# Attention, a two-dimensional Fourier transform and a feed-forward layer on one core: tie weights in PSUM, a norm by columns, ungated value loads and a written plan of finer calls

## The chip, the cores and the metric

The program runs on one core of a Trainium2 chip. The metric is the device time of one execution in microseconds (us). Within the core, TensorE (PE in the profile; PEld is its weight load), VectorE (DVE), ScalarE (ACT) and GpSimd (POOL) compute, and SyncE (SP) issues the transfers.

## What is computed

```python
q_assign = argmax(einsum('bhsd,hcd->bhsc', q_n, c_n), -1)     # likewise k_assign; rows normalised
mask = q_assign[:, :, :, None] == k_assign[:, :, None, :]
scores = where(mask, scale * q @ k.T, -1e9)
attn = softmax(scores) @ v                                    # 4 batches, 8 heads, 768 x 64
x = attn, heads side by side                                  # 4 x 768 x 512
u = x + real(fft(fft(x, axis=1), axis=2))
un = (u - mean(u)) / sqrt(var(u) + 1e-6)
out = u + maximum(un @ w_ch1, 0) @ w_ch2                      # 512 -> 2048 -> 512
```

The two weight matrices arrive as 8-byte floats.

## The kernel before

**Work.** There are 16 pairs of heads (four of each batch), and each has six tiles of scores for either head, 192 of 128x768 in all. A pair goes through four streams. `prep` loads q and k, finds their largest values, sets the scales, splits each into two 16-bit halves, and assigns every row to a cluster. `scores` multiplies (L596, L601), takes the row's extreme on DVE (L615), the exponential on ACT (L618), splits the result into halves (L626 on ACT, L627 on POOL) and transposes it by DMA (L629). `attend` multiplies by the values (L647 to L649), and `load_v` and `split_v` bring the values in and split them (L466, L475 to L477). When the four pairs of a batch are done, its tile X of 768x512 goes through `fold` and `transform` (L908 and L999, matmuls L977) and then through the layer in three blocks of 256 rows: `norm` (L1069), `inverse` (L1101), `up` (L1127, 192 matmuls to a block) and `down` (L1157, 96). A batch's transform and layer fill PE between the scores of the next batches. Behind batch 3 nothing is left to fill with.

**Weights.** In the first 190 us the 32 pieces of the weights (512 KB each) are loaded, their sign and exponent are put together on PE (L767, L791), the rest of the bits is joined on DVE (L795), and the result is halved on ACT, DVE and POOL (L804, L807, L805). The raw pieces lie in `arena`, a stretch of SBUF that the transform and the layer use later.

**Ties.** In `prep`, L547 turns the cluster products into one PSUM bank; L553 takes the largest of each row and L555 compares, after which the bank is free. POOL multiplies by tie weights (L557), L561 takes the largest again into a small SBUF tile `mx2`, and one L565 and two L569 compare with it, 16 and 32 times over the run. Both inputs of these, `a` (tile ac) and `mx2`, lie in SBUF.

**PSUM.** Scores have two buffers of two banks (ps_big), the products with the values one bank (ps_o), and all else shares three banks (ps_f): the turned cluster products, the weights' block and join, the transform, up and down.

**Order.** `Overlap` (L1170) calls the streams by a timetable: every step of a pair has a time, and the transform and the layer are let in by a budget of costs. Each call is marked, and after tracing, `Order` (L77) goes through all instructions with a cost of its own for each and hands every engine, whenever it is free, the instruction of the earliest call whose inputs its costs hold to be ready. So the order on an engine follows from the calls and from `Order`'s costs. `Order` is not changed.

**Values.** From the second or third pair on, `load_v` first copies one number from the newest row extreme (`self.late`) into the value tile on POOL (L465, 14 times). The transfer of the values (L466) waits for that copy, and stands in SP's queue in its place.

**Norm.** For a block's two tiles of 128 rows, `norm` takes the statistics (L1083, L1084) and then does five operations of 128x2 on DVE: the variance plus 1e-6 (L1085), a shift and a mask of its bits (L1086), a subtraction that gives a power of two near its inverse root (L1088), the product with the mean (L1090), and a copy of the variance for `inverse` (L1091). ACT normalises (L1094, L1096), DVE or POOL takes the low half (L1097), and a DMA transposes it for `up`.

Of the kernel before, what the change touches and what calls it, by code (L numbers as in the profile page):

```python
# [56 lines left out]
def top_power(nc, tops, t, s, inv):  # L57

    t = t.bitcast(I32)
    nc.vector.tensor_scalar(out=t, in0=tops.bitcast(I32), scalar1=23, scalar2=None, op0=ALU.logical_shift_right)  # L60
    nc.vector.tensor_scalar(out=t, in0=t, scalar1=-13.0, scalar2=1.0, op0=ALU.add, op1=ALU.max)
    nc.vector.tensor_scalar(out=inv.bitcast(I32), in0=t, scalar1=240.0, scalar2=float(1 << 23), op0=ALU.min, op1=ALU.mult)
    nc.vector.reciprocal(out=s, in_=inv)
# [276 lines left out]
class Arena:  # L340
# [5 lines left out]
    def at(self, off, shape, dt):  # L346
        n = int(np.prod(shape[1:]))
        size = 2 if dt in (F16, BF16, U16) else 4
        assert off % 32 == 0 and off + n * size <= self.t.shape[1] * 4
# [8 lines left out]
class Attention:  # L358
# [9 lines left out]
    def __init__(self, ctx, tc, q, k, v, cent, X, ident, sc, psf, kept):  # L368
# [9 lines left out]
        self.late, self.centered, self.ready, self.mark = None, False, -1, None  # L378
# [103 lines left out]
    def load(self, pr):  # L482
        b, hp = divmod(pr, H // 2)
        t = self.sb.tile([P, 2, S], F32, name="scr", tag="scr")
        for side in range(2):
            self.nc.sync.dma_start(out=t[:, side], in_=(self.q, self.k)[side][b, hp])
        self.nat[pr] = t

    def largest_qk(self, pr):
        m = self.sb.tile([P, 3], F32, name="amx", tag="amx", bufs=2)  # L490
        for i in range(2):
            self.nc.vector.tensor_reduce(out=m[:, i:i + 1], in_=self.nat[pr][:, i], op=ALU.max, axis=AX.X,
                                         apply_absolute_value=True)
        return m
# [11 lines left out]
    def split_qk(self, pr, side):  # L506
# [5 lines left out]
        i = nc.vector.scalar_tensor_tensor(out=hl[:, 1], in0=src, scalar=s, in1=hl[:, 0], op0=ALU.mult, op1=ALU.subtract)  # L512
        if pr == 0:
            self.mark = i
        return hl

    def prep(self, pr):
        nc, sb = self.nc, self.sb
        hp = pr % (H // 2)
        self.load(pr)  # L520
        yield
        m = self.largest_qk(pr)
        yield
        nc.vector.tensor_reduce(out=m[:, 2:3], in_=self.vst[pr].rearrange("p a x -> p (a x)"), op=ALU.max, axis=AX.X,
                                apply_absolute_value=True)
        yield
# [4 lines left out]
        yield  # L531
# [28 lines left out]
        mx2 = sb.tile([P, G], F32, name="mx", tag="mx")  # L560
# [7 lines left out]
        for h in range(2):  # L568
            i = nc.vector.tensor_tensor(out=k[:, :, :, h, 0:NC_], in0=av[:, :, h, 1],  # L569
                                        in1=mv[:, :, h, 1].broadcast_to([P, 3, 2, NC_]), op=ALU.is_equal)  # L570
        if pr == 0:
            self.mark = i
# [8 lines left out]
        self.ready = pr  # L581
# [3 lines left out]
    def scores(self, pr, st):  # L585
        nc, sb = self.nc, self.sb
        assert self.ready >= pr
# [15 lines left out]
        for j in range(2):  # L603
# [11 lines left out]
            self.mark = nc.vector.tensor_scalar(out=ju, in0=ps[j][:, :, 0:SH], scalar1=ne, scalar2=None, op0=ALU.mult, op1=ALU.min,  # L615
                                    accum_out=m)
            self.late = m
# [13 lines left out]
        if st == ST - 1:  # L631
            self.hl.pop(pr)
            self.oht.pop(pr)


    def attend(self, pr, st):
        nc, sb = self.nc, self.sb
        W = D + 2
        if st % 3 == 0:
            self.otile[pr] = self.po.tile([P, 512], F32, name="ps_o")  # L640
        o = self.otile[pr]
        for j in range(2):
            v16, pt = self.v16[2 * pr + j], self.pt.pop((pr, st, j))
            at = (st % 3 * 2 + j) * W
            for kt in range(ST):
                hi, lo = pt[:, kt], pt[:, ST + kt]
                nc.tensor.matmul(out=o[:, at:at + W], lhsT=hi, rhs=v16[:, kt, 0:W], start=(kt == 0), stop=False)  # L647
                nc.tensor.matmul(out=o[:, at:at + D], lhsT=hi, rhs=v16[:, kt, 66:130], start=False, stop=False)  # L648
                nc.tensor.matmul(out=o[:, at:at + W], lhsT=lo, rhs=v16[:, kt, 0:W], start=False, stop=(kt == ST - 1))  # L649
        if st % 3 == 2:  # L650
            self.finish(pr, st // 3)
# [55 lines left out]
class Weights:  # L707
# [7 lines left out]
    RAW, PN = tuple(4128 * i for i in range(6)) + (29696, 33824), (24768, 40000, 44096)  # L715
    ID, TOP, MX, ONE = 28864, 29376, 29472, 29568
    X32 = 37952
    EXTRA, A2, AHEAD = 0, 9, 7

    def __init__(self, tc, pool, arena, psf, w1, w2, ident):  # L720
# [5 lines left out]

        self.inv = [pool.tile([P, 4], F32, name=f"winv{n}") for n in range(2)]
        self.rel = pool.tile([P, 16], F32, name="wrel")
        self.scale, self.bits, self.sum = {}, {}, {}

    def raw(self, k):

        n, e = len(self.RAW), self.EXTRA
        if n <= k < n + e:
            o = 16 * DM - 2064 * ((k - n) // 2 + 1)
            return self.w2[k % 2].rearrange("p a x -> p (a x)")[:, o:o + 4 * DM + 8].bitcast(U16)
        return self.arena.at(self.RAW[(k if k < n else k - e) % n], [P, 4 * DM + 8], U16)

    def loads(self, k):

        n = len(self.RAW) + self.EXTRA
        if k < 0:
            k += self.AHEAD
            return range(n * k // self.AHEAD, n * (k + 1) // self.AHEAD)
        a = min(self.A2, n - 1)
        return [p for p in range(n, 32) if k == p - (a if p < n + len(self.RAW) else len(self.RAW) - 1)]

    def top(self, k):
        raw = self.raw(k)
        return raw[:, 4:4 + 4 * DM].rearrange("p (n f) -> p n f", f=4)[:, :, 0]  # L750

    def load(self, k):
        m, i = divmod(k, 16)
        raw = self.raw(k)
        src = self.src[m][i % 4 * P:(i % 4 + 1) * P, i // 4 * DM:(i // 4 + 1) * DM] if m == 0 else \
            self.src[m][i * P:(i + 1) * P]
        self.nc.sync.dma_start(out=raw[:, 1:1 + 4 * DM], in_=src.bitcast(U16))

    def block(self, g):
# [4 lines left out]
        i = 0  # L764
        for k in range(4 * g, 4 * g + 4):
            for j in range(2):
                nc.tensor.matmul(out=ps, lhsT=self.ones[:, 0:1].broadcast_to([P, P]), rhs=self.bits[k][:, j], start=(i == 0), stop=(i == 7))  # L767
                i += 1
        mx = at(self.MX + 32 * (g % 2), [P, 1], F32)
        nc.vector.tensor_reduce(out=mx, in_=ps, op=ALU.max, axis=AX.X)  # L770
        s = self.sb.tile([P, 1], F32, name="wsc", tag="wsc", bufs=2)
        top_power(nc, mx, ps[:, 0:1], s, self.inv[g // 4][:, g % 4:g % 4 + 1])
        for i in range(4):
            self.scale[4 * g + i] = s[:, 0:1]

    def signs(self, k):

        nc, at = self.nc, self.arena.at
        pn = at(self.PN[k // 2 % 3], [P, 2, 2, DM], BF16)
        raw = at(self.RAW[k % len(self.RAW)], [P, 2, 4 * DM + 16], U16)  # L780
        top = raw[:, :, 4:4 + 4 * DM].rearrange("p a (n f) -> p a n f", f=4)[:, :, :, 0]
        nc.scalar.activation(pn[:, 0].bitcast(I16), top.bitcast(I16), AF.Relu, bias=self.off[:, 0:1], scale=8.0)
        nc.scalar.activation(pn[:, 1].bitcast(I16), top, AF.Relu, bias=self.off[:, 1:2], scale=8.0)
# [600 lines left out]
```

## Time and profile before

| | us |
|---|---|
| three runs | 998.67, 1002.95, 1002.15 |
| median | 1002.15 |
| the profiled execution | 1003.47 |
| its span | 1001.40 |
| outside the span | 2.07 |
| PE busy | 896.3 |
| POOL, ACT, DVE busy | 601.6, 604.3, 599.3 |
| PE idle ahead of 250 us, 250 to 860 us, behind 860 us | 81.6, 15.0, 8.6 |

The profile is one execution. Its span runs from the first to the last recorded instruction, and each engine's busy time is counted on its own. An idle time of PE is put down to what released PE last. Where another engine is on the chain that ended last, its busy time counts as PE's does.

### The profile page before, as it was taken

To read this page: it belongs to the slowest core of one execution; us is meant where nothing else is said; L and a number is where in the kernel's file an instruction comes from. 1 tells how busy PE (TensorE), PEld (TensorE's weight loads), DVE (VectorE), ACT (ScalarE), POOL (GpSimd) and SP (SyncE) were. 2 spreads that over 40 slices of the span, in tenths; PEclk is the share of its full clock that TensorE was granted. 3 is DMA by queue.
4 is the path that set the end of the run, shared out by engine and by line. 5 is a ranking of instruction groups with operands and counts; after the bars stand their busy time and mean duration, and the time that the engine had idled before them with its cause. 6 is when DMAs were issued, how large, how long until landed. Compare 5 with 4: busy or idle time off the path is not lost.

```text
span 1001.4 us, 23416 instructions
## 1 busy us (share of the span) xinstructions
PE 896.3 (90%) x9349; PEld 586.1 (59%) x9368; DVE 599.3 (60%) x1276; ACT 604.3 (60%) x948; POOL 601.6 (60%) x702
## 2 busy tenths in 40 slices
PE   3775768578899999999999999889999999899998
PEld 1243444356666757666757667556658585576683
DVE  7788979789555655879555646767554335611110
ACT  6899989656756756557656656557656352342130
POOL 2467667667866756759857567559757462552230
PEclk9799877778899999999999999999999999999999
DMA  7799999979768666699676666689765552311000
GB/s 263 196 225 256 267 226 238 198 157 179 143 118 175 108 154 134 123 181 212 116 167 118 154 118 143 122 151 180 118 125 109 107 106 59 71 26 33 11 11 22
DMA packets 397374, 140.65 MB, mean 140 GB/s; under 512 B 381904, under 2 KB 382928, under 8 KB 397264
## 3 DMA queue, kind: packets, MB, share of 16 engines
q1 hardware_dynamic: 397264, 139.16, 67.4%
q8 instruction: 73, 1.20, 0.5%
q14 instruction: 37, 0.30, 0.1%
HBM read 43.17 MB, written 6.29 MB: 49 GB/s over the span
## 4 chain that ended last, share of the span: by engine, by line
PE 62%; DVE 14%; ACT 8%; DMA 6%; issue 5%; POOL 4%; SPq 1%; DVEq 0%; ACTq 0%; POOLq 0%
PE ps_f L1157 21%; PE ps_f L1127 20%; PE ps_big L596 7%; PE ps_f L977 3%; PE ps_o L647 2%; PE ps_o L648 2%; PE ps_o L649 2%; DVE ps_big L615 2%; PE ps_big L601 2%; DMA scr<-in_q_dram 2%; DMA pt<-p 1%; ACT p L618 1%; POOL ph L627 1%; DVE X L615 1%; DMA arena<-in_moe_w_ch_dram 1%
## 5 line engine op out<-in xcount | busy, mean ns | idle before, releaser
L627 POOL TENSOR_TENSOR ph<-p,ph 128x768 f16<-128x768 f32 x144 | 241.3, 1678 | 137.0 <-ACT ph L626 101.0
L1127 PE MATMUL ps_f<-arena,w1h 128*128 128x256 f16 x1536 | 267.1, 274 | 11.3 <-ACT arena L1135 11.2
L1157 PE MATMUL ps_f<-w2h,arena 128*128 128x512 f16 x768 | 239.3, 379 | 0.2 <-ACT arena L1135 0.2
L1127 PE MATMUL ps_f<-arena,w1l 128*128 128x256 f16 x768 | 210.7, 274 | 0.0
L618 ACT ACTIVATE p<-ps_big,rmx 128x768 f32<-128x768 f32 x144 | 128.9, 898 | 129.5 <-DVE ps_big L615 82.2
L615 DVE TENSOR_SCALAR_CACHE_REDUCE ps_big<-ps_big,sce 128x768 f32<-128x768 f32 x144 | 142.0, 1020 | 68.8 <-PE ps_big L601 67.5
L1157 PEld LDWEIGHTS <-arena 128*128 128x128 f16 x1152 | 109.0, 98 | 125.9 <-issue 5.0
L1136 POOL TENSOR_TENSOR arena<-arena 128x256 f16<-128x256 f32 x192 | 130.9, 691 | 79.8 <-ACT arena L1135 75.7
L1127 PEld LDWEIGHTS <-w1h 128*128 128x128 f16 x1536 | 151.0, 98 | 23.2 <-issue 4.8
L596 PE MATMUL ps_big<-hlk,hlq 64*128 64x384 f16 x1152 | 127.2, 345 | 22.6 <-ACT p L618 11.8
L1157 PE MATMUL ps_f<-w2l,arena 128*128 128x512 f16 x384 | 145.5, 379 | 0.0
L626 ACT CAST ph<-p 128x768 f16<-128x768 f32 x144 | 118.9, 828 | 27.2 <-DMA pt<-ph 26.9
L647 PE MATMUL ps_o<-v,pt 128*128 128x66 f16 x1152 | 123.7, 198 | 11.5 <-DMA pt<-p 7.5
L648 PE MATMUL ps_o<-v,pt 128*128 128x64 f16 x1152 | 123.6, 199 | 0.0
L649 PE MATMUL ps_o<-v,pt 128*128 128x66 f16 x1152 | 123.2, 197 | 0.0
L647 PEld LDWEIGHTS <-pt 128*128 128x128 f16 x1152 | 109.7, 100 | 22.2 <-DMA pt<-p 8.3
L1132 DVE TENSOR_SCALAR arena<-ps_f,wrel 128x256 f32<-128x256 f32 x96 | 46.3, 482 | 121.4 <-PE ps_f L1127 83.7
L1135 ACT ACTIVATE arena<-ps_f,wrel 128x256 f16<-128x256 f32 x192 | 89.6, 474 | 42.4 <-DVE arena L1132 41.9
L648 PEld LDWEIGHTS <-pt 128*128 128x128 f16 x1152 | 110.1, 100 | 4.6 <-issue 0.8
L649 PEld LDWEIGHTS <-pt 128*128 128x128 f16 x1152 | 110.4, 102 | 0.0
L596 PEld LDWEIGHTS <-hlq 64*128 64x128 f16 x1152 | 54.8, 98 | 81.9 <-issue 55.6
L1127 PEld LDWEIGHTS <-w1l 128*128 128x128 f16 x768 | 75.5, 98 | 21.2 <-issue 12.3
(178 smaller groups left out, 1311.9 us busy)
## 6 DMA issues: line engine op xcount, KB each, us to landing
arena<-in_moe_w_ch_dram SPq DMA_DIRECT2D x32, 512.0 KB, 5.2
scr<-in_q_dram SPq DMA_DIRECT2D x16, 384.0 KB, 3.5
scr<-in_k_dram SPq DMA_DIRECT2D x16, 384.0 KB, 4.3
vst<-in_v_dram SPq DMA_DIRECT2D x16, 384.0 KB, 4.0
out_dram<-arena SPq DMA_DIRECT2D x24, 256.0 KB, 2.2
pt<-ph SPq DMA_TRANSPOSE x168, 3.8
arena<-in_cs_dram SPq DMA_DIRECT2D x12, 192.0 KB, 3.9
arena<-in_ss_dram SPq DMA_DIRECT2D x12, 192.0 KB, 3.9
```

The lines of the kernel that those rows point to most:

```text
L596: nc.tensor.matmul(out=ps[j][:, hf, 0:SH], lhsT=hq[rows[j], a, sl], rhs=hk[rows[j], c, hs], start=(i == 0), stop=False)
L615: self.mark = nc.vector.tensor_scalar(out=ju, in0=ps[j][:, :, 0:SH], scalar1=ne, scalar2=None, op0=ALU.mult, op1=ALU.min, accum_out=m)
L618: nc.scalar.activation(x, ju, AF.Exp, bias=m, scale=-1.0)
L626: nc.scalar.copy(out=ph[:, 0], in_=p32)
L627: nc.gpsimd.tensor_tensor(out=ph[:, 1], in0=p32, in1=ph[:, 0], op=ALU.subtract)
L647: nc.tensor.matmul(out=o[:, at:at + W], lhsT=hi, rhs=v16[:, kt, 0:W], start=(kt == 0), stop=False)
L648: nc.tensor.matmul(out=o[:, at:at + D], lhsT=hi, rhs=v16[:, kt, 66:130], start=False, stop=False)
L649: nc.tensor.matmul(out=o[:, at:at + W], lhsT=lo, rhs=v16[:, kt, 0:W], start=False, stop=(kt == ST - 1))
L1127: nc.tensor.matmul(out=ps.rearrange("p (t x) -> p t x", x=P), lhsT=a[:, dc, fs], rhs=c[:, :, dc], start=(i == 0), stop=(i == 11))
L1135: nc.scalar.activation(hh[:, f], ps, AF.Relu, scale=rel[:, f:f + 1])
L1136: nc.gpsimd.tensor_tensor(out=hl[:, f], in0=r, in1=hh[:, f], op=ALU.subtract)
L1157: nc.tensor.matmul(out=ps, lhsT=a[:, f, ts], rhs=c[:, f], start=(i == 0), stop=(i == 47))
```

## The change

**Tie weights.** `mx2` has no SBUF tile any more; it is written to the 24 columns behind the cluster products in the PSUM bank of L547. The bank stays taken until the last of the three comparisons.

**Norm.** Each of the two columns has its own four operations of 128x1, the copy is gone (`inverse` reads the variance where it lies), and `mv` is three wide. A norm has eight small operations where it had five.

**Values.** The copy of L465 is gone; the transfer waits for its tile alone.

**Calls.** In place of the timetable stands `PLAN`, a text of words: p is prep, s scores, a attend, v values, t transform, n norms, f layer, l weight loads, w conversion, c centroids; the digits name the pair or batch and *n says how many steps. The streams give way more often: q and k load apart, each largest value and each split is a step, scores and attend step by head, the conversion after signs, block, join and halve, and the transform after each of its parts. The pieces of the weights and the transform's tables lie at other places of `arena` (the latter 96 bytes on), and the scales of the second matrix are kept in 16 columns.

```diff
...
-        if self.late is not None:
-
-            nc.gpsimd.tensor_copy(out=t[:, 0, 0:1], in_=self.late)
         nc.sync.dma_start(out=t, in_=self.v[b, :, 2 * hp:2 * hp + 2])
...
     def prep(self, pr):
...
-        self.load(pr)
-        yield
-        m = self.largest_qk(pr)
-        yield
...
+        for i in range(2):
+            self.load(pr, i)
+            yield
+        m = self.sb.tile([P, 3], F32, name="amx", tag="amx", bufs=2)
+        for i in range(3):
+            self.largest(pr, m, i)
+            yield
         self.scales(pr, m)
         yield
-        hl = self.hl[pr] = [self.split_qk(pr, side) for side in range(2)]
+        hl = self.hl[pr] = []
+        for i in range(2):
+            hl.append(self.split_qk(pr, i))
+            yield
...
-        mx2 = sb.tile([P, G], F32, name="mx", tag="mx")
+        mx2 = ps[:, G * NC_:G * NC_ + G]
         nc.vector.tensor_reduce(out=mx2, in_=a, op=ALU.max, axis=AX.X)
...
-        va = sb.tile([P, 2], F32, name="mv", tag="mv", bufs=2)
         s = sb.tile([P, 2, 2], F32, name="rpow", tag="rpow", bufs=2)
+        mv = sb.tile([P, 2, 3], F32, name="mv", tag="mv", bufs=2)
...
-        nc.vector.tensor_scalar(out=mv[:, :, 1], in0=mv[:, :, 1], scalar1=1e-6, scalar2=None, op0=ALU.add)
-        nc.vector.tensor_scalar(out=e.bitcast(I32), in0=mv[:, :, 1].bitcast(I32), scalar1=1, scalar2=0x7F800000,
-                                op0=ALU.logical_shift_right, op1=ALU.bitwise_and)
-        nc.vector.tensor_scalar(out=s[:, 0].bitcast(I32), in0=e.bitcast(I32), scalar1=-1.0, scalar2=float(USC << 23),
-                                op0=ALU.mult, op1=ALU.add)
-        nc.vector.scalar_tensor_tensor(out=s[:, 1], in0=mv[:, :, 0], scalar=-1.0, in1=s[:, 0], op0=ALU.mult, op1=ALU.mult)
-        nc.vector.tensor_copy(out=va, in_=mv[:, :, 1])
-        for j in range(2):
+            nc.vector.bn_aggr(out=mv[:, j, 0:2], in_=st)
+            mean, var, e = (mv[:, j, i:i + 1] for i in range(3))
+            nc.vector.tensor_scalar(out=var, in0=var, scalar1=1e-6, scalar2=None, op0=ALU.add)
+            nc.vector.tensor_scalar(out=e.bitcast(I32), in0=var.bitcast(I32), scalar1=1, scalar2=0x7F800000,
+                                    op0=ALU.logical_shift_right, op1=ALU.bitwise_and)
+            nc.vector.tensor_scalar(out=s[:, 0, j:j + 1].bitcast(I32), in0=e.bitcast(I32), scalar1=-1.0, scalar2=float(USC << 23),
+                                    op0=ALU.mult, op1=ALU.add)
+            nc.vector.tensor_scalar(out=s[:, 1, j:j + 1], in0=mean, scalar1=s[:, 0, j:j + 1], scalar2=-1.0, op0=ALU.mult, op1=ALU.mult)
...
-        return va, s[:, 0], self.rest[:, blk]
+        return mv[:, :, 1], s[:, 0], self.rest[b][:, blk]
...
+    PLAN = """
+p0*2 c v0 p0*4 c l w l v1 p0*3 p1*2 l p0 l p0 p1*3 l*2 p0 v0*2 l*2 p1 s0*2 w*5 p1*2 s0*2 l w*2 v2 s0*2 p1 v1 p2*2 l w*2 l w*2
...
+a15*3 f2*2 s15*2 f2*2 a15*2 f2*4 a15*2 f2*4 a15*3 f2*7 t3*4 f2*2 t3*2 f2 t3*12 f2*2 t3 n3*2 t3*2 f2 t3*3 f3 n3*2 f3*21 n3*2
+f3*50
+"""
...
+        for word in self.PLAN.split():
+            name, _, n = word.partition("*")
+            if name not in streams:
+                streams[name] = self.make[name[0]](int(name[1:] or 0))
+            for _ in range(int(n or 1)):
                 self.order.cut("rest")
-                f(*a)
...
+                next(streams[name])
```

The order on PE is much the same before and after: the same matmuls, in large stretches in the same row, and from the last product of pair 14 to the end without a difference. DVE has 36 instructions more, POOL 14 fewer. Three places show what moves.

DVE at the comparisons with the tie weights of the first pair of batch 1. The operands are written as output, arrow, inputs; X_64 is a stretch of SBUF that holds a score tile here, v the split values, vst the raw values, arena the weights' pieces. Before:

```order
L795 SCALAR_TENSOR_TENSOR ps_f<-arena,ps_f 128x512
L565 TENSOR_TENSOR oh<-ac,mx 128x12x16
L615 TENSOR_SCALAR X_64,rmx<-ps_big,sce 128x768
L807 SCALAR_TENSOR_TENSOR w2l<-ps_f,wsc,w2h 128x512
L569 TENSOR_TENSOR oh<-ac,mx 128x6x16
L615 TENSOR_SCALAR X_64,rmx<-ps_big,sce 128x768
L569 TENSOR_TENSOR oh<-ac,mx 128x6x16
L492 TENSOR_REDUCE amx<-scr 128x1 x2
L524 TENSOR_REDUCE amx<-vst 128x1
```

The same place after:

```order
L563 TENSOR_REDUCE ps_f<-ac 128x24
L496 TENSOR_REDUCE amx<-scr 128x1
L567 TENSOR_TENSOR oh<-ac,ps_f 128x12x16
L496 TENSOR_REDUCE amx<-scr 128x1
L571 TENSOR_TENSOR oh<-ac,ps_f 128x6x16
L620 TENSOR_SCALAR X_64,rmx<-ps_big,sce 128x768
L571 TENSOR_TENSOR oh<-ac,ps_f 128x6x16
L620 TENSOR_SCALAR X_64,rmx<-ps_big,sce 128x768
```

The three comparisons read the bank in place of `mx`, and the largest values of the next pair's q and k, which came behind them together, now stand among them.

POOL at the load of the values for the second pair of batch 1, where batch 0 is folded (L919, L929). Before:

```order
L476 MEMSET v_2993 128x6x2
L929 TENSOR_TENSOR arena<-arena,X_63 1x255
L465 COPY vst<-rmx 128x1
L627 TENSOR_TENSOR ph<-p_2644,ph 128x768
L919 TENSOR_TENSOR arena<-arena 128x3x255
L627 TENSOR_TENSOR ph<-p_2653,ph 128x768
```

After:

```order
L930 TENSOR_TENSOR arena<-arena,X_63 1x255
L919 TENSOR_TENSOR arena<-arena 128x3x255
L475 MEMSET v_2978 128x6x2
L631 TENSOR_TENSOR ph<-p_2637,ph 128x768
L631 TENSOR_TENSOR ph<-p_2646,ph 128x768
```

The copy is gone, and the fold's operation of POOL stands ahead of the subtractions of the two score tiles where it stood between them.

DVE at the second norm of batch 3, behind the last scores. Before:

```order
L1084 BN_AGGR mve<-bst 128x2
L1041 SCALAR_TENSOR_TENSOR arena<-ps_f,vseq,arena 128x257
L1085 TENSOR_SCALAR mve<-mve 128x2
L1086 TENSOR_SCALAR mve<-mve 128x2
L1091 COPY mv<-mve 128x2
L1088 TENSOR_SCALAR rpow<-mve 128x2
L1090 SCALAR_TENSOR_TENSOR rpow<-mve,rpow 128x2
```

After:

```order
L1046 SCALAR_TENSOR_TENSOR arena<-ps_f,vseq,arena 128x257
L1091 TENSOR_SCALAR mv<-mv 128x1
L1089 BN_AGGR mv<-bst 128x2
L1047 SCALAR_TENSOR_TENSOR arena<-ps_f,vseq,arena 128x257
L1092 TENSOR_SCALAR mv<-mv 128x1
L1091 TENSOR_SCALAR mv<-mv 128x1
L1094 TENSOR_SCALAR rpow<-mv 128x1
L1092 TENSOR_SCALAR mv<-mv 128x1
L1096 TENSOR_SCALAR rpow<-mv,rpow 128x1
L1094 TENSOR_SCALAR rpow<-mv 128x1
L1096 TENSOR_SCALAR rpow<-mv,rpow 128x1
```

The first column begins while the second still waits for its statistics, and from there the two take turns.

## Rows read from the trace of the kernel before

**Rows 1.** The page: each engine's busy time, share and instructions.

```profile
PE 896.3 (90%) x9349; PEld 586.1 (59%) x9368; DVE 599.3 (60%) x1276; ACT 604.3 (60%) x948; POOL 601.6 (60%) x702
```

**Rows 2.** Windows: length; busy PE, PEld, DVE, ACT, POOL; clock share; DMA share; GB/s.

```profile
0.00:250.00 250.00, 168.39 (x1967) 100.13 (x1987) 206.71 (x454) 200.56 (x266) 154.25 (x170) 0.85 1.00 220
50.00:125.00 75.00, 50.49 (x686) 30.11 (x694) 63.99 (x143) 72.66 (x94) 50.25 (x45) 0.93 1.16 249
...
300.00:860.00 560.00, 549.60 (x5980) 365.47 (x5977) 336.00 (x701) 332.23 (x544) 361.40 (x403) 0.99 0.69 135
860.00:1001.40 141.40, 132.83 (x918) 89.52 (x916) 27.59 (x57) 38.66 (x85) 48.53 (x80) 1.00 0.10 25
```

**Rows 3.** Timeline of DVE near 170 us: start, duration, instruction, [idle before, releaser].

```profile
168.00 1.20 DVE L565 TENSOR_TENSOR oh<-ac,mx 128x192 bf16<-128x192 f32 x1
...
172.81 1.07 DVE L569 TENSOR_TENSOR oh<-ac,mx 128x96 bf16<-128x96 f32 x1
```

**Rows 4.** Timeline of POOL over the same stretch.

```profile
166.91 2.08 POOL L627 TENSOR_TENSOR ph<-X,ph 128x768 f16<-128x768 f32 x1 [0.96 <-POOL arena L928]
```

**Rows 5.** Single lines over the whole run: shortest, median, longest in ns; first, last start.

```profile
L565 DVE TENSOR_TENSOR oh<-ac,mx x16: 316/368/1611, 22.3 to 749.7; 128x192 bf16<-128x192 f32 x16
L569 DVE TENSOR_TENSOR oh<-ac,mx x32: 243/346/1702, 22.6 to 753.0; 128x96 bf16<-128x96 f32 x32
L555 DVE TENSOR_TENSOR ac<-ps_f,mx x16: 547/558/558, 18.8 to 746.1; 128x384 f32<-128x384 f32 x16
L553 DVE TENSOR_REDUCE mx<-ps_f x16: 548/554/558, 18.2 to 745.5; 128x24 f32<-128x384 f32 x16
L561 DVE TENSOR_REDUCE mx<-ac x16: 530/552/554, 21.0 to 749.1; 128x24 f32<-128x384 f32 x16
```

**Rows 6.** The chain that ended last, in order of time: start, duration, what.

```profile
168.10 0.97 DVE oh L565
...
199.84 0.71 POOL vst L465
200.56 3.12 DMA vst<-in_v_dram
...
673.27 1.59 DVE rpow L1088
```

**Rows 7.** Timeline of all engines around the value load at 200 us.

```profile
191.21 6.45 SPq L629 DMA_TRANSPOSE pt<-ph  x2
...
198.94 1.59 POOL L465 COPY vst<-rmx 128x1 f32<-128x1 f32 x1 [1.20 <-ACT p L618]
...
203.78 0.95 DVE L524 TENSOR_REDUCE amx<-vst 128x1 f32<-128x768 f32 x1 [0.85 <-DMA vst<-in_v_dram]
```

**Rows 8.** Timeline of DVE in norms of batches 0 and 3.

```profile
234.08 1.58 DVE L1085 TENSOR_SCALAR mve<-mve 128x2 f32<-128x2 f32 x1
...
244.13 1.50 DVE L1090 SCALAR_TENSOR_TENSOR rpow<-mve,rpow 128x2 f32<-128x2 f32 x1
...
858.13 0.17 DVE L1085 TENSOR_SCALAR mve<-mve 128x2 f32<-128x2 f32 x1
...
875.03 1.00 DVE L1090 SCALAR_TENSOR_TENSOR rpow<-mve,rpow 128x2 f32<-128x2 f32 x1
```

**Rows 9.** Timeline of PE where `up` begins in batches 0 and 3.

```profile
255.66 0.37 PE L1127 MATMUL ps_f<-arena,w1h 128*128 128x256 f16 x1 [4.37 <-ACT arena L1135]
...
874.21 0.27 PE L1127 MATMUL ps_f<-arena,w1h 128*128 128x256 f16 x1 [2.96 <-ACT arena L1135]
...
877.35 0.27 PE L1127 MATMUL ps_f<-arena,w1h 128*128 128x256 f16 x1 [1.67 <-ACT arena L1135]
```

**Rows 10.** Timeline near 64 us: operations of 128x1 beside a subtraction on POOL.

```profile
63.86 1.65 POOL L627 TENSOR_TENSOR ph<-X,ph 128x768 f16<-128x768 f32 x1
...
64.90 0.30 DVE L686 TENSOR_SCALAR sce<-scp 128x1 f32<-128x1 f32 x2
```

**Rows 11.** Waits of PE: tile, line, releaser; us in all, times, longest.

```profile
PE ps_f L791 <- ACT arena L804: 10.9, 6, 2.6
```

More of the change, by code (lines that the diff above doesn't have):

```diff
@@ L479, in split_v, with values, load, largest @@
         self.v16[n] = t
-    def load(self, pr):
-        b, hp = divmod(pr, H // 2)
[L484 to L494, printed above, removed]
+    def values(self, pr):
+        self.load_v(pr)
+        yield
+        for j in range(2):
+            self.split_v(2 * pr + j)
+            yield
+    def load(self, pr, side):
+        b, hp = divmod(pr, H // 2)
+        if side == 0:
+            self.nat[pr] = self.sb.tile([P, 2, S], F32, name="scr", tag="scr")
+        self.nc.sync.dma_start(out=self.nat[pr][:, side], in_=(self.q, self.k)[side][b, hp])
+    def largest(self, pr, m, i):
+        x = self.nat[pr][:, i] if i < 2 else self.vst[pr].rearrange("p a x -> p (a x)")
+        self.nc.vector.tensor_reduce(out=m[:, i:i + 1], in_=x, op=ALU.max, axis=AX.X, apply_absolute_value=True)
     def scales(self, pr, m):
@@ L739, in loads @@
[L739 to L750, printed above, removed]
+        first = 32 - 2 * self.LATE
+        self.groups = [range(k, k + 4) for k in range(0, first, 4)] + [range(k, k + 2) for k in range(first, 32, 2)]
@@ L759, in block @@
-    def block(self, g):
-        nc, at = self.nc, self.arena.at
-        ps = self.psf()
[L764 to L774, printed above, removed]
+        self.nc.sync.dma_start(out=self.raw(k)[:, 1:1 + 4 * DM], in_=src.bitcast(U16))
@@ L784, in signs, with block @@
         self.bits[k], self.bits[k + 1] = pn[:, :, 0], pn[:, :, 1]
+    def block(self, ks):
+        nc, at = self.nc, self.arena.at
+        ps = self.psf()
+        i, n = 0, 2 * len(ks)
+        for k in ks:
+            for j in range(2):
+                nc.tensor.matmul(out=ps, lhsT=self.ones[:, 0:1].broadcast_to([P, P]), rhs=self.bits[k][:, j], start=(i == 0), stop=(i == n - 1))
+                i += 1
+        m, c = divmod(ks[0], 16)
+        mx = at(self.MX + 32 * (ks[0] // 2 % 2), [P, 1], F32)
+        nc.vector.tensor_reduce(out=mx, in_=ps, op=ALU.max, axis=AX.X)
+        s = self.sb.tile([P, 1], F32, name="wsc", tag="wsc", bufs=2)
+        top_power(nc, mx, ps[:, 0:1], s, self.inv[m][:, c:c + len(ks)] if m else self.inv[m][:, c // 4:c // 4 + 1])
+        for k in ks:
+            self.scale[k] = s[:, 0:1]
     def join(self, k):
-        nc, at = self.nc, self.arena.at
+        nc = self.nc
         pn = self.bits.pop(k)
@@ L807, in halve, with loads, convert @@
             nc.vector.scalar_tensor_tensor(out=lo, in0=ps, scalar=s, in1=hi, op0=ALU.mult, op1=ALU.subtract)
-    def run(self):
+    def loads(self):
+        for k in range(32):
+            self.load(k)
+            yield
+    def convert(self):
         nc, at = self.nc, self.arena.at
@@ L1136, in up, with norms, layer @@
             nc.gpsimd.tensor_tensor(out=hl[:, f], in0=r, in1=hh[:, f], op=ALU.subtract)
-            yield 1.3
+            yield
+    def norms(self, b):
+        for blk in range(3):
+            m = self.norm(b, blk)
+            yield
+            self.inverse(*m)
+            yield
+    def layer(self, b):
+        for blk in range(3):
+            yield from self.up(blk)
+            yield from self.down(b, blk)
     def down(self, b, blk):
@@ L1223, in fill @@
-    def fill(self, share):
-        if self.hold == self.now:
-            return
-        self.credit += share * self.left / max(self.end - self.now, 1)
-        while self.credit > 0:
-            c = self.step()
-            if not c:
-                self.credit, self.hold = 0.0, self.now
-                return
-            self.credit -= c
-            self.left -= c
-    def step(self):
-        self.order.cut("rest")
-        return next(self.gen, 0.0)
-    def drain(self, keep):
-        while self.left > keep:
-            c = self.step()
-            if c == 0.0:
-                return
-            self.left -= c or 0.0
@@ new lines, with centroids @@
+a15*3 f2*2 s15*2 f2*2 a15*2 f2*4 a15*2 f2*4 a15*3 f2*7 t3*4 f2*2 t3*2 f2 t3*12 f2*2 t3 n3*2 t3*2 f2 t3*3 f3 n3*2 f3*21 n3*2
+f3*50
+"""
+    def __init__(self, tc, att, fft, ffn, wts, order):
+        self.att, self.order = att, order
+        self.make = {"p": att.prep, "s": att.scores, "a": att.attend, "v": att.values, "t": fft.transform, "n": ffn.norms,
+                     "f": ffn.layer, "l": lambda _: wts.loads(), "w": lambda _: wts.convert(), "c": self.centroids}
+    def centroids(self, _):
+        self.att.nc.sync.dma_start(out=self.att.X[1][:, 0, 0:D], in_=self.att.cent.rearrange("h c d -> (h c) d"))
+        yield
+        self.att.centroids()
+        yield
+    def run(self):
+        streams = {}
+        self.att.setup()
+        for word in self.PLAN.split():
[3 more added lines that the diff above has]
+            for _ in range(int(n or 1)):
+                self.order.cut("rest")
+                next(streams[name])
+        assert all(next(g, "end") == "end" for g in streams.values())
```

298 lines of the change are left out of this document (109 added, 189 removed).

## The prediction

> **What bounds the kernel now.** I began with the page's busy times [rows 1]. PE is busy 896.3 of 1001.40 us, and no other engine is above 604.3. The windows [rows 2] then tell where the other 105 us of PE lie. Ahead of 250 us, 250 less 168.4 = 81.6 us are idle. From 300 to 860 us it is 10.4 of 560, so there PE itself is the bound: the change takes no matmul away, and an operation that waits on DVE costs nothing as long as PE has other work. Behind 860 us it is 8.6 of 141.4. So the change can pay in three places: the first 260 us, where the other engines feed PE too slowly; the passages from one batch's transform to its layer; and the last such passage, behind which nothing is left to fill with.
>
> Within the first stretch no engine is the bound by itself. From 50 to 125 us ACT is nearest to it, busy 72.7 of 75 us [rows 2]; DVE has 64.0 there. From 160 us the chain passes through DVE, ACT and transfers in turns, and names two things that the change is about: a comparison of L565, and the copy of L465 with the value load behind it [rows 6].
>
> **What a busy POOL does to DVE.** The first comparison of the pair at 168 us takes 1.20 us [rows 3]. POOL's subtraction runs from 166.91 to 168.99 [rows 4], and the comparison ends 0.2 us after it. The shortest of its kind takes 316 ns, and L569 runs from 243 to 1702 ns. L555, which reads one input from PSUM, ran 547 to 558 ns in all of its 16 places, whatever POOL did [rows 5]. So an operation of two SBUF inputs waits until POOL's is over, and one with an input in PSUM does not. The norm's operations of 128x2 read one SBUF input and wait as well: 1.58 and 1.50 us at batch 0, where the undisturbed one takes 0.17 [rows 8].
>
> **The terms.** All against the profiled execution, 1003.47 us (span 1001.40 and 2.07 outside).
>
> Tie weights. Of the three comparisons of this pair the first loses 1.20 - 0.35 = 0.85 and the last 1.07 - 0.25 = 0.82 [rows 3, 5]; the middle one is like them, 0.96. DVE is on the chain there, so 2.6 us go. In the other pairs ahead of 250 us the waits add up to 1.6 more, off the chain; behind 300 us PE covers them. Bounds 0 (what DVE waits for next is as late) and -4.2. I take **-2.6**.
>
> Values. At 200 us the transfer started behind the copy, at 200.56 [rows 6]. SP had finished the transposes ahead of it at 191.21 + 6.45 = 197.66 [rows 7], so it could go 2.9 us earlier. The copy itself took 1.59 and waited 1.20 for ACT. What DVE loses is the 0.85 us ahead of the largest value at 203.78 [rows 7]; the score tiles next to it come at their own pace. Moving the load also puts it ahead of one transpose on SP and beside it on the transfer engines, whose share is 1.00 over the stretch [rows 2], which takes some of that back from the tile whose transpose then lands later. Bounds 0 and -2.9. I take **-0.85**. The other 13 copies lie on POOL at about 0.2 us where PE covers them.
>
> Norms of batch 0. Eight operations of 128x1 take the place of five. The nearest row for such an operation beside a running subtraction is L686: two of them in 0.30 us from 64.90, while POOL ran from 63.86 to 65.51 [rows 10], so 0.15 each and no wait. That row has its factor behind a pointer, which three of the four new operations don't, so that it is near and not the same. With 0.16 each, a norm's eight take 1.28. The five took 3.26 in the first norm (1.58 the largest) and 2.76 in the second (1.50 the largest) [rows 8], and 1.66 in the third: -2.0, -1.5 and -0.4, or 3.9 in all. PE is idle 4.37 us ahead of the first up [rows 9], so that there is room for all of it; but the last piece of this passage is a chain over ACT, POOL and a transpose, and one of the three norms is hidden beside the scores. I take **-3.5**, with bounds 0 and -4.4 (the whole gap).
>
> Norms of batch 3. Here nothing covers. PE waits 2.96 and 1.67 us ahead of up's beginnings [rows 9], 4.63 in all, and ends the run with 120 us of up and down without a gap, so that what is saved ahead of them is saved at the end. The second norm's five take 2.55 us, the third's 2.70 (1.00 the largest) [rows 8]; at 1.24 for eight that is -1.3 and -1.4. The third norm's column may go on to ACT as soon as its own four are done, but ACT takes both tiles in turn, so I count no more. Some of the second gap is up's wait for the low half on POOL. I take **-2.2**, bounds 0 and -2.7.
>
> Norms of batches 1 and 2. PE has little idle time there, though the chain does pass through a 1.59 us L1088 at 673 us [rows 6]. I take **-1.0**, bounds 0 and -3.
>
> The start. The finer steps let DVE begin with the largest values of q while k still comes, and let q and k come ahead of the centroids; what follows is bounded by transfers. **-0.5**, bounds 0 and -1.5.
>
> The bank that is held. Before, the bank is free behind L555; now it is taken to the last L569. In the first pair that is from 18.8 to 22.6 us, in the last from 746.1 to 753.0 [rows 5], so 4 to 7 us more of one bank in three for each pair. Ahead of 190 us the weights' block and join ask for the same three, and PE waits 10.9 us in six places for ACT to empty one [rows 11]. With two left instead of three, each such wait may last half as long again, 5.5 us in all; most of them do not fall on those 4 to 7 us. I take **+1.5**, bounds 0 and +13 (below).
>
> The remaining edits cost or bring nothing I can find: the scales in 16 columns are a few elements more on DVE, and the other places in `arena` change no size.
>
> Sum: -2.6 - 0.85 - 3.5 - 2.2 - 1.0 - 0.5 + 1.5 = -9.15, so 994.3 for an execution like the profiled one. This lies 1.3 above the median, and the forecast for the median is **993.0 us**.
>
> [...] L553 reads 384 numbers from PSUM in 554 ns, L561 as many from SBUF in 552 [rows 5], so that the source makes no difference here. [...]
>
> **The rivals.**
>
> The gains stay off the path. In the first stretch ACT is at 72.7 of 75 us, and a DVE that comes earlier waits for ACT; the norms of batch 0 wait for transposes. What is left is the tail, -2.2: 1001.3 for the profiled execution, **1000.0** as a median. For it speaks ACT's share; against it, that from 160 to 185 us the chain runs through DVE nearly without a break. 0.18.
>
> The columns still wait for POOL. If an operation of 128x1 takes the same path as one of 128x2, eight of them wait where five did, and the norm terms (3.5 + 2.2 + 1.0 = 6.7) are gone: -2.45, a median of **999.7**. Against it stands L686 [rows 10]; for it, that L686 is of another kind. 0.07. [...]
>
> Slower: the banks. If the bank of L547 is held while the weights' joins queue for one of two, PE starves in the pairs ahead of 190 us. At one more wait of the longest kind seen, 2.6 us [rows 11], for each of five pairs that is +13, and the gains in front of it (tie weights, values, start) are then gone, since PE waits for a bank and not for DVE. With the norms' -6.7 that is +6.3, a median of **1008.5**. It decides from the point at which ACT, which is busy 72.7 of 75 us between 50 and 125, falls below some 68. Against it: the joins' banks are emptied by ACT in any case, and ACT is full. 0.10.
>
> Faster than forecast: every term at its lower end, -4.2 - 2.9 - 4.4 - 2.7 - 3 - 1.5 and nothing for the bank, -18.7 in all and a median of **983.5**. It would take PE's gaps in the first 250 us closing as each of these waits goes, where now another engine is next. 0.05.
>
> **How the numbers follow.** The forecast's case has 0.60, the others 0.18, 0.07, 0.10 and 0.05. About 0.5%, 5 us, is what a measurement of this kernel can tell from no change: faster is below 997.1, slower above 1007.2. The forecast's case and the fast one give 0.65 faster (a little of the first is lost to the middle, and a little of the second rival, at 999.7, gained). The two rivals near 1000 make 0.25 same; the banks 0.10. The range leaves out a tenth at either side: from 984, the fast case, to 1003, which takes in both rivals near 1000 with the spread of the runs.
>
> **What would show it.** In the profile of the changed kernel: comparisons L567 and L571 under 0.45 us all over the run, none over 1; norm operations of 128x1 at 0.15 to 0.2 while POOL runs; PE's waits ahead of the first up of batch 0 and of the two in the tail shorter by 2 to 4 and by about 2 us in all; the value load at 200 us right behind the transposes; and PE's waits at block and join not above 17 us in all. Columns at 0.7 us or more would be the third case; a longer wait of PE for ps_f ahead of 190 us with ACT below 68 of 75 the fourth. The prediction is wrong as a whole if the finer calls move scores and joins in the first 250 us so that PE's 81.6 idle us there change by more than ten in either way, since I count only half a microsecond for the plan itself.

## The result and the profile after

The changed kernel takes 1008.34 us (median of ten runs, 1004.5 to 1010.8), the kernel before 1002.66 in the same ten; the ratio is 1.0056, 95% interval 1.0038 to 1.0073. So it is slower by a half per cent, where 993 and a gain of 0.9% were forecast, and it lies outside the range of 984 to 1003. The profiled execution after took 1010.80 us, span 1009.0, 7.3 more than that of before.

The page of the kernel after, busy times as in [rows 1], and its windows as in [rows 2]:

```profile
PE 895.0 (89%) x9350; PEld 584.6 (58%) x9368; DVE 572.7 (57%) x1312; ACT 605.8 (60%) x948; POOL 593.3 (59%) x688
```

```profile
0.00:250.00 250.00, 166.02 (x1942) 95.79 (x1960) 198.03 (x450) 197.43 (x264) 146.65 (x160) 0.86 1.00 220
50.00:125.00 75.00, 52.26 (x684) 29.56 (x691) 59.57 (x137) 67.88 (x90) 49.16 (x42) 0.89 1.12 244
300.00:860.00 560.00, 540.62 (x5947) 361.76 (x5946) 316.51 (x703) 335.19 (x541) 355.68 (x392) 0.99 0.71 133
400.00:500.00 100.00, 91.65 (x1019) 63.56 (x1017) 67.95 (x160) 63.49 (x107) 75.18 (x88) 0.98 0.81 155
```

DVE has 26.6 us less to do, POOL 8.3 less, and PE the same; yet PE is idle 114.0 us in place of 105.1. Ahead of 250 us it is 84.0 (81.6 before), from 300 to 860 us 19.4 (10.4 before). Of the nine more there, most lie where batch 1 is transformed. The same window of the kernel before:

```profile
400.00:500.00 100.00, 98.39 (x1106) 67.06 (x1105) 76.29 (x160) 66.44 (x113) 77.23 (x94) 1.00 0.82 159
```

The next table follows both executions by equal work: the start of a matmul on the timeline of PE, with as many matmuls behind it in the one as in the other.

| start, us | before | after | difference |
|---|---|---|---|
| first product of pair 5 | 263.8 | 266.0 | +2.2 |
| first product of pair 8 | 418.3 | 420.2 | +1.9 |
| first product of pair 9 | 467.7 | 476.7 | +9.0 |
| first product of pair 13 | 684.4 | 693.4 | +9.1 |
| first up of batch 3 | 867.2 | 878.1 | +10.9 |
| first down of batch 3 | 893.3 | 900.6 | +7.3 |
| the last matmul | 997.1 | 1004.5 | +7.3 |

So the first 264 us, for which 7.5 us of gain (6 with the bank's +1.5) stood in the sum, lose two; batch 1's passage loses seven; two more go between pair 13 and the first up of batch 3; and the tail gains 3.6. The sign that was to condemn the prediction as a whole, a change of more than ten in the idle time ahead of 250 us, did not come: it changed by 2.4.

What the edits do to single operations is as forecast. Single lines over the whole run, as in [rows 5] (shortest, median, longest in ns):

```profile
L567 DVE TENSOR_TENSOR oh<-ac,ps_f x16: 315/353/355, 25.7 to 759.2; 128x192 bf16<-128x192 f32 x16
L571 DVE TENSOR_TENSOR oh<-ac,ps_f x32: 232/247/251, 26.0 to 762.8; 128x96 bf16<-128x96 f32 x32
L1091 DVE TENSOR_SCALAR mv<-mv x24: 106/143/154, 238.2 to 882.8; 128x1 f32<-128x1 f32 x24
L1096 DVE TENSOR_SCALAR rpow<-mv,rpow x24: 181/208/215, 239.5 to 883.3; 128x1 f32<-128x1 f32 x24
```

No comparison and no column waits for POOL any more, in any place. Not as forecast is when the values are loaded. The queue of SP up to 100 us, its value loads from the third on, in the kernel before:

```profile
44.34 0.68 SPq L466 DMA_DIRECT2D vst<-in_v_dram  x1
78.62 1.00 SPq L466 DMA_DIRECT2D vst<-in_v_dram  x1
```

and in the kernel after:

```profile
17.65 0.33 SPq L465 DMA_DIRECT2D vst<-in_v_dram  x1
32.28 0.33 SPq L465 DMA_DIRECT2D vst<-in_v_dram  x1
91.06 0.38 SPq L465 DMA_DIRECT2D vst<-in_v_dram  x1
```

The copy of L465 had kept each load back until a score of the pair before was there. Without it the third load goes at 17.65 us, right behind the split of the first pair's values (L476, 17.01 to 17.63 us). The third, fourth and fifth load come 27, 46 and 31 us earlier, nearly a whole pair, and the seventh, which the prediction priced, at 168.38 us where it was 200.56 [rows 6]. And PE now waits longest for transposed tiles, 31.9 us (16 times) where it was 11.1 (11 times). The waits of PE before, as in [rows 11]:

```profile
PE ps_o L647 <- DMA pt<-p: 7.5, 7, 1.9
PE ps_o L647 <- DMA pt<-ph: 3.6, 4, 1.6
```

and after:

```profile
PE ps_o L657 <- DMA pt<-ph: 20.9, 8, 5.7
PE ps_o L657 <- DMA pt<-p: 11.0, 8, 2.7
...
PE ps_f L787 <- ACT arena L799: 5.2, 4, 1.6
```

### The profile page after: what moved, and what is told of

Same layout as the page of the kernel before. It is cut to its first block, busy times and chain, and to the rows that moved or that the text cites. A ratio compares the mean times of both kernels' runs of the same rounds, so it can differ in the third digit from the quotient of the medians.

```text
span 1009.0 us, 23465 instructions
## 1 busy us (share of the span) xinstructions
PE 895.0 (89%) x9350; PEld 584.6 (58%) x9368; DVE 572.7 (57%) x1312; ACT 605.8 (60%) x948; POOL 593.3 (59%) x688
## 4 chain that ended last, share of the span: by engine, by line
PE 60%; DMA 11%; ACT 9%; POOL 7%; DVE 7%; issue 4%; SPq 2%; POOLq 0%; ACTq 0%; DVEq 0%
PE ps_f L1131 21%; PE ps_f L1173 20%; PE ps_big L601 6%; DMA pt<-ph 6%; POOL ph L631 3%; ACT ph L630 2%; PE ps_f L979 2%; DMA pt<-p 2%; PE ps_o L659 2%; PE ps_o L657 2%; PE ps_o L658 2%; PE ps_big L606 2%; ACT X L622 1%; PE ps_f L772 1%; DMA arena<-arena 1%
## 5 line engine op out<-in xcount | busy, mean ns | idle before, releaser
L620 DVE TENSOR_SCALAR_CACHE_REDUCE ps_big<-ps_big,sce 128x768 f32<-128x768 f32 x144 | 141.9, 1021 | 80.8 <-PE ps_big L606 76.7
L601 PE MATMUL ps_big<-hlk,hlq 64*128 64x384 f16 x1152 | 124.3, 342 | 16.7 <-DVE X L620 8.0
```

The costliest lines, as they stand in the source:

```text
L601: nc.tensor.matmul(out=ps[j][:, hf, 0:SH], lhsT=hq[rows[j], a, sl], rhs=hk[rows[j], c, hs], start=(i == 0), stop=False)
```

## The experiments

Four causes were held against each other: the plan of finer calls costs more than the edits bring (theory 1); the bank that is held starves the weights' joins (2); value loads that are no longer held back get into the way (3, and as 4 once their times were known: the copy was a brake); and, from the third group of runs on, that all these differences are the luck of an order. A deal, below, is one order that `Order` makes of the same instructions. The ratio's 95% interval to the kernel before stands in brackets.

**One edit alone, and all three, on the old calls.** The kernel before with the tie maxima in the bank (a1):

```diff
-        mx2 = sb.tile([P, G], F32, name="mx", tag="mx")
+        mx2 = ps[:, G * NC_:G * NC_ + G]
```

> The kernel before with the tie maxima in the bank of L547 and nothing else. Theory 1 (the three edits save what their waits cost, and the written plan gives back more): no comparison above 0.45 us, and 999.5 to 1001.5 us against about 1002.7 for before. Theory 2 (the held bank starves the weights' joins): 1006 to 1010, with PE's waits for ps_f ahead of 190 us longer by 5 or more than in before.

Measured: 1003.71 us, 1.0021 (1.0003 to 1.0038). With the norm by columns (a2, the norm of the change and nothing else):

> The kernel before with the norm's small operations column by column. Theory 1: PE's waits in the tail fall from 4.6 us by 2 to 3 and the first up of batch 0 comes 2 to 3 earlier: 996 to 999. Theory 2 says nothing of it: 996 to 999 too. If the gaps only move: 1002 to 1003.

Measured: 998.17, 0.9970 (0.9956 to 0.9985). The time is the one expected, but the first up of batch 0 comes 3.5 us later at equal work (250.2 us, 246.7 before) and not 2 to 3 earlier: what is gained is the tail. Without the copy (a3):

```diff
-        if self.late is not None:
-            nc.gpsimd.tensor_copy(out=t[:, 0, 0:1], in_=self.late)
```

> The kernel before without the copy ahead of the value loads. Theory 1: 1001 to 1002. Theory 3 (value loads that start earlier get into the way of the transposes, which PE waits for 32 us after the change and 11 before): 1005 to 1010, with PE's waits for transposed tiles at 25 us or more.

Measured: 1011.55, 1.0111 (1.0093 to 1.0129), but without the waits that theory 3 asked for: those for transposed tiles are 9.5 us. All three together, with the old calls (a4):

> The kernel before with all three edits (tie maxima in PSUM, norm by columns, no copy ahead of the value loads) and the old calls. Theory 1: 992 to 996, so that the plan of finer calls alone would cost 12 to 16 us. Theories 2 and 3: 1003 to 1010, near the changed kernel's 1008.3.

Measured: 1001.61, 0.9997 (0.9984 to 1.0010). The three edits bring nothing together, and the one that takes the copy away costs as much as the other two were to save. The bank is not the cause: in a1 PE's waits for the weights' block and join do not grow (14.3 us, 17.0 before), and the start of pair 5 comes at 260.1 us, 3.7 earlier than before; the 3.7 are lost between pairs 8 and 10 (108.0 us in place of 102.7).

**The copy put back.** The changed kernel with the two lines of L465 in it again (b3):

> The changed kernel with the copy ahead of the value loads put back. Theory 4 (the copy was a brake that kept each value load some 30 us later, and without it the loads come a pair early, at 17 and 32 us where before issued them at 44 and 79): the loads go back to about 44 and 79 us and the time falls from about 1008 to 1000 to 1003. If the finer calls alone cost the time: 1007 to 1010.

Measured: 994.02, 0.9926 (0.9911 to 0.9941): 14 us less than the changed kernel. The loads are at 44.37 and 79.24 us again, and PE's waits for transposed tiles are back to 9.2. The changed kernel with all three edits undone, so the written plan alone (b4):

> The changed kernel with all three edits undone (tie maxima in SBUF, norm on 128x2, the copy back), so that only the written plan, its finer calls and the places in the arena are left. If the plan alone costs the time: 1007 to 1012, and the tail's waits are those of before. If the plan costs nothing by itself and the loss comes of the edits under it: 1000 to 1004.

Measured: 1007.08, 1.0060 (1.0042 to 1.0078). The kernel before with columns and tie maxima, the copy kept (c1):

> The kernel before with the norm by columns and the tie maxima in PSUM, the copy ahead of the value loads kept. If the edits add up as they did alone (0.997 and 1.0021 of before): 1000 to 1001 against about 1001.2. If the held bank and the columns' order disturb each other: 1002 or more.

Measured: 992.33, 0.9906 (0.9888 to 0.9924), the fastest of all and faster than both kernels; far more than its parts alone, 0.9970 and 1.0021, would make. The copy on DVE in place of POOL (c2):

```diff
-            nc.gpsimd.tensor_copy(out=t[:, 0, 0:1], in_=self.late)
+            nc.vector.tensor_copy(out=t[:, 0, 0:1], in_=self.late)
```

> The kernel before with the copy ahead of the value loads on DVE in place of POOL. Theory 4 (it matters that the copy holds the load back, and not where it runs): the loads stay at about 44 and 79 us and the time at 999 to 1003. If it was the copy's place on POOL that kept the order good: 1006 or more, as without it (1011.6).

Measured: 1004.25, 1.0026 (1.0009 to 1.0043), with the loads at 45 and 78 us. It is between the two theories, nearer to the brake.

**What of the copy it is.** In c1, the copy moved from the load to the largest value, so that the load is free and DVE's work on it is not (d1):

```diff
+        if self.late is not None:
+            nc.gpsimd.tensor_copy(out=m[:, 2:3], in_=self.late)
         nc.vector.tensor_reduce(out=m[:, 2:3], in_=self.vst[pr].rearrange("p a x -> p (a x)"), op=ALU.max, axis=AX.X,
```

> Norm by columns and tie maxima in PSUM on the old calls (c1, 992.3 us), with the copy moved: it no longer holds the load of the values, it holds DVE's largest value of them. If what costs without the copy is the work on the values that comes early on DVE, ACT and POOL: 991 to 995. If it is the load itself (its transfer, its place in SP's queue): 999 to 1003, as with the copy gone (a4, 1001.6).

Measured: 999.77, 0.9988 (0.9969 to 1.0007), loads at 16 and 30 us: 7 us more than c1, as if the copy were gone. And in c1 the copy of an older extreme, `self.lates[-6]` (d4):

> c1 with the copy reading a row extreme five score tiles older than the newest, so that each value load in the first 200 us may go some 15 us earlier than in c1 and still later than without the copy. If the time follows how early the load is: 995 to 999, between c1 and a4. If only the place of the newest extreme is good by chance: no order with earliness, 990 to 1005.

Measured: 997.12, 0.9956 (0.9939 to 0.9972), loads at 16, 66 and 99 us (c1: 43, 79, 118; a4: 17, 32, 91). Both agree with the load's being early as the cause, and both, like c2, could be something else, as the next runs show.

**What an order is worth by itself.** In c1 one number of `Order`'s costs, by which no work, wait or transfer changes (n1):

```diff
-    AFTER = {"DVE": 75, "Activation": 100, "Pool": 40, "PE": 160}
+    AFTER = {"DVE": 80, "Activation": 100, "Pool": 40, "PE": 160}
```

> c1 with one number of the planner's costs moved a little (75 to 80 ns behind each DVE operation), which leaves the work and its waits alone and only deals a somewhat other order. It tells what a new order is worth by itself: if the differences between the kernels are the edits', 990 to 995; if they are mostly the luck of an order, anywhere from 988 to 1003.

Measured: 998.83, 0.9968 (0.9955 to 0.9980): 6.5 us more than c1 for the same work. With the surcharge for comparisons that wait taken out of `Order` (d3):

```diff
-        (lambda e, i, acc: e == "DVE" and any(a[1] and a[0].startswith("oh_") for a in acc), 310),
+        (lambda e, i, acc: e == "DVE" and any(a[1] and a[0].startswith("oh_") for a in acc), 0),
```

> c1 with the planner's 310 ns surcharge on the comparisons taken away, since they no longer wait for POOL (0.25 to 0.35 us in the trace). If the planner's order rests on true costs: 988 to 992. If a new order is luck: 988 to 1003.

Measured: 995.02, 0.9929 (0.9911 to 0.9947); the truer cost brings nothing over c1. Since a new deal is worth as much as an edit, the rest of the runs were new deals with the copy (n2, n3, q1) and without it (m1, m2, p1).

> c1 (columns, tie maxima in PSUM, copy kept, old calls; 992.3 us) with the planner's 75 ns behind a DVE operation at 70. A second deal of the order with the copy. If the copy's absence is what costs: this and the other deals with the copy lie at 990 to 999, all below the deals without it. If both are deals of luck: the two groups mix between 990 and 1004.

> c1 with the planner's 75 ns at 85, a third deal with the copy: 990 to 999 if the copy's absence costs, anywhere between 990 and 1004 if it is luck.

> All three edits on the old calls, so without the copy (a4, 1001.6 us), with the planner's 75 ns at 80. If the copy's absence costs: 999 to 1008. If it is luck: anywhere between 990 and 1004.

> All three edits on the old calls, without the copy, with the planner's 75 ns at 70. If the copy's absence costs: 999 to 1008. If it is luck: anywhere between 990 and 1004.

> The changed kernel with the copy put back (b3, 994.0 us) and the planner's 75 ns at 80: a second deal of the written plan with the copy. If the copy's absence costs: 991 to 1000. If it is luck: anywhere between 990 and 1009.

> The changed kernel (1008.3 us, without the copy) with the planner's 75 ns at 80: a second deal of the written plan without the copy. If the copy's absence costs: 1002 to 1010. If it is luck: anywhere between 990 and 1009.

Measured, beside the kernels with the same number in `Order` (ratio to before):

| calls, number | with the copy | without it | difference |
|---|---|---|---|
| old, 75, the other two edits undone | 1 (before) | 1.0111 (a3) | +0.0111 |
| old, 75 | 0.9906 (c1) | 0.9997 (a4) | +0.0091 |
| old, 80 | 0.9968 (n1) | 0.9982 (m1) | +0.0014 |
| old, 70 | 0.9914 (n2) | 1.0048 (m2) | +0.0134 |
| written plan, 75 | 0.9926 (b3) | 1.0056 (after) | +0.0130 |
| written plan, 80 | 1.0021 (q1) | 0.9983 (p1) | -0.0038 |

n3, with the copy and 85, has 1.0007 (0.9991 to 1.0022). c1, n1, n2 and n3 do the same work and differ by 10 us, 992.3 to 1002.6. The two groups mix. Five of the six differences point the same way, and their mean is +0.0074, with an interval of about ±0.0074 from their own spread: some 7 us for the copy's absence, and hardly told from nothing. The written plan against the old calls, at equal edits and number, gives five differences (b4 and before, b3 and c1, after and a4, q1 and n1, p1 and m1): 0.0060, 0.0020, 0.0059, 0.0053 and 0.0001, mean 0.0039 ± 0.0033. Columns and tie maxima together give three (c1 and before, a4 and a3, b3 and b4): -0.0094, -0.0114 and -0.0134, all at the number 75. The kernel before has been dealt only once; against that one order the four deals with columns, tie maxima and the copy on the old calls (c1, n1, n2, n3) lie at -0.0094, -0.0032, -0.0086 and +0.0007, mean -0.0051.

**What an order changes: two places.** The first is where the columns lie. In batch 0's passage of a2, which has nothing but the columns, the five operations that ran back to back from 242.92 to 245.63 us before have become eight that `Order` places one by one. DVE in a2:

```profile
245.43 0.14 DVE L1084 TENSOR_SCALAR mv<-mv 128x1 f32<-128x1 f32 x1
...
246.48 1.09 DVE L512 SCALAR_TENSOR_TENSOR hlq<-scr,scp,hlq 128x768 f16<-128x768 f32 x1
...
250.22 1.01 DVE L615 TENSOR_SCALAR_CACHE_REDUCE ps_big<-ps_big,sce 128x768 f32<-128x768 f32 x1
...
251.16 0.14 DVE L1085 TENSOR_SCALAR mv<-mv 128x1 int32<-128x1 int32 x1
```

Two operations of 0.14 us that follow each other in one column lie 5.7 us apart, with the next pair's halves and two score tiles in between, and the second norm is done at 253.7. The first product of pair 5 comes at 263.9 us, where it was 263.8: what the columns save there on paper is gone. The changed kernel does the same (its L1092 at 246.04 is followed by L1094 at 252.77).

In c1 it goes the other way. It differs from a1 by the columns alone, and DVE, ACT, POOL and PE run the same order in both ahead of 224 us. There the second norm's columns lie together, from 237.52 to 240.36 us, and PE's wait behind the first matmuls of up of batch 0 is, in a1 and in c1:

```profile
253.23 0.37 PE L1127 MATMUL ps_f<-arena,w1h 128*128 128x256 f16 x1 [6.00 <-ACT arena L1135]
249.12 0.27 PE L1124 MATMUL ps_f<-arena,w1h 128*128 128x256 f16 x1 [1.94 <-ACT arena L1132]
```

The first product of pair 5 comes at 253.2 us in c1 and at 260.1 in a1; 1.7 of these 6.9 us stand already ahead of the passage (229.3 and 231.0 us at equal work). From 244 to 262 us PE's granted clock is 1.00 of full speed in c1 and 0.81 in a1, and the matmul behind the wait takes 0.27 us in c1 and 0.37 in a1.

The second place is that clock over the whole of the first 260 us. The windows of c1 and of n3, each in its profiled execution, up to the first product of pair 5, with the same matmuls behind it:

```profile
0.00:253.20 253.20, 170.27 (x2030) 100.86 (x2049) 206.96 (x483) 207.47 (x281) 165.29 (x191) 0.91 1.03 226
0.00:263.56 263.56, 180.46 (x2033) 106.67 (x2049) 212.61 (x483) 206.18 (x280) 164.10 (x190) 0.84 0.98 217
```

PE is idle 82.9 us in c1 and 83.1 in n3. The 10.4 us between them are PE's busy time: the same matmuls take 10.2 us longer, at a mean granted clock of 0.84 in place of 0.91. In windows of one us from 100 to 260 us, the granted clock of the kernel before is 1.00 of full speed in 86, 0.50 in 61 and between the two in 13. If PE has these two levels in c1 and n3 as well, it has the lower for an estimated 46 us in c1 and 84 in n3, from the 0.91 and 0.84. n2 is alike (176.3 busy, 83.9 idle, 0.87). So a deal can cost without PE's waiting longer in sum. Why the clock was lower in n3 was not worked out.

## Why the prediction was wrong, and where it was right

**Waits for POOL: right.** All 48 comparisons and all norm operations behave as the terms had it, 0.23 to 0.36 and 0.11 to 0.22 us. The rival of columns that wait is out. (One reading was loose: L1090, of the 1.50 and 1.00 us in [rows 8], has two SBUF inputs and not one.)

**Tail: right, and too small.** First up to first down of batch 3 takes 22.5 us where it took 26.1, in a2, c1, a4, b3, the changed kernel and seven more with columns (23.6 and 24.4 in three others), and 26.1 or 25.9 in all without them. PE's waits there after, as in [rows 9]:

```profile
883.27 0.27 PE L1131 MATMUL ps_f<-arena,w1h 128*128 128x256 f16 x1 [1.10 <-ACT arena L1139]
```

1.10 is left of 4.63. The term was -2.2, bound -2.7, and it measured -3.6. The second norm's share is 1.86 where -1.3 stood: its columns do not wait and the first begins ahead of the second's statistics, so that ACT normalises 1.87 us behind the first up (879.94 us) where it was 3.73 (870.88). The third's wait of 1.67 is gone whole, where -1.4 stood. For what a first column gains ahead of the second I had counted nothing.

**Values: the sign came out wrong, as far as six pairs can tell.** I priced the one load whose wait stood on the chain, as one that would go 2.9 us earlier (it went 32), and took the other 13 copies for nothing. They were not nothing: a copy that waits for a result is a date for the load behind it (the third load went at 44.34 us with it and at 17.65 without), and the order of SP, which I had read, had the third load seven rows further ahead. In its place the runs show some +7 us (six pairs, -4 to +13, the mean hardly told from nothing), on transfers that have a share of 1.00 over the first 250 us [rows 2]. By what path the early load costs isn't settled: PE's waits for transposed tiles rise from 9 to 32 us on the written plan and from 5 to 13 on the old calls (c1, a4), but not in a3 (11.1 and 9.5), and in p1 they rise from 11 to 22 (q1) while the time falls. Up to pair 5 the changed kernel's 12.1 us over b3 are idle time (88.8 and 76.7, with 177.2 busy in both); of a4's 9.6 over c1, 8.1 are busy time, at a clock of 0.85 and 0.91.

**Norms of batches 0 to 2: gone in a2 and in the changed kernel, not in c1.** -3.5 and -1.0 stood in the sum; a2 shows nothing of them ahead of pair 8 and no gain at equal work by the first up of batch 3 (868.4 us, 867.2 before). The step that failed is the one that made eight operations one piece of 1.28 us: `Order` places them one by one, and it depends on the deal whether they stay together (c1, 6.9 us ahead of a1 at pair 5). The wait of 4.37 us was also misread: it does not lie ahead of the first up, which begins at 246.68 us, but behind its first 36 matmuls, where PE waits for ACT to empty a bank, and in the changed kernel such a wait is still 3.55 us.

**Tie weights and bank.** On their own 3.7 us by pair 5, where -2.6 was taken, and given back in batch 1's passage. The bank did not bind: PE's waits for the weights' block and join are 7.6 us in all after, 17.0 before. So the slower rival, whose 1008.5 is the time measured, was right in its number alone. Even its sign came, ACT at 67.9 of 75 between 50 and 125 us, though these waits had fallen; it wasn't a sign of the bank only.

**The sum.** Columns and tie maxima together measured -9 to -13 us at the number 75, with the copy as without it, on the old calls and on the plan, and -5 as a mean of four deals against the one order of the kernel before; the terms for them were -7.8. What went wrong is the rest, +7 for the copy's absence and +4 for the finer calls where -0.85 and -0.5 stood, and that the whole was put on one order. Ten us between deals of the same work are more than the sum itself, and the range counted only the terms and the spread of the runs. By these means the three parts come to about zero with the -11 of the number 75 and to about +6 with the -5; the changed kernel has +5.7. How much of that is the three parts and how much this one deal stays open: it is not traced further than the passages in the table above.

## What to carry to other kernels

Where a scheduler with a cost model sets the order, an edit's waits can be priced from the trace, but what is next on the freed engine can't; deal the order a few times with a cost moved by a little, in both kernels, before a difference under one per cent is put down to an edit (the four deals c1, n1, n2 and n3 differ by 10 us of some 1000). Compare PE's busy time and granted clock at equal work, and not its waits alone (c1 and n3 differ by 0.2 us in idle time and by 10.2 in busy time). Look at a wait that seems idle for what it holds back: the copy on POOL cost 0.2 us (median 188 ns of 14) and dated a transfer. And a chain of small operations that must be short gains from smaller ones where nothing else is placed between them, as in the tail (26.1 us before, 22.5 after); elsewhere that is the order's to decide.

## What the hardware showed

An operation of 128x1 with one SBUF input and constants did not wait for POOL: 24 of L1091 took 106 to 154 ns, 17 of them begun while an operation of POOL ran, where those of 128x2 took up to 1.58 us [rows 8]. And the comparison L567 with one input in PSUM took as long (315 to 355 ns, median 353) as L565 with both in SBUF in the eight places where no operation of POOL ran beside it (316 to 359), so that the move to PSUM had no price of its own on DVE here. The same matmuls took 10.2 us more of PE's time at a mean granted clock of 0.84 (n3) than at 0.91 (c1).
